# Issuing the second half-batch's v gathers in pairs, each pair behind a copy on GpSimd

## The chip, the core and the metric

The kernel runs on one core of a Trainium2 chip. The metric is the device time of one execution in microseconds (us), lower is better; the time of the kernel before is the median of three timed executions. The engines are named as in the profile: PE is TensorE (PEld its weight loads), DVE is VectorE, ACT is ScalarE, POOL is GpSimd, SP is SyncE.

## The reference, cut to what matters

Three parts run one after the other: an attention with decay, a mixture of experts, and a gated layer with a spatial mix. Only the last one is touched:

```python
def _moe2_ref(x, w_in, w_spatial, b_spatial, w_out):     # x: 4 x 576 x 512
    h = np.maximum(x @ w_in, 0.0)
    u, v = (h[..., :512], h[..., 512:])
    mu = np.mean(v, axis=-1, keepdims=True)
    var = np.mean((v - mu) ** 2, axis=-1, keepdims=True)
    v_n = (v - mu) / np.sqrt(var + 1e-06)
    v_s = np.einsum('ts,bsd->btd', w_spatial, v_n) + b_spatial[None, :, None]
    gated = u * v_s
    return gated @ w_out
```

## The kernel before

The tokens leave the experts sorted by expert. `project` computes u and v for 18 blocks of 128 sorted tokens and writes them to the DRAM tensors `z_u` and `z_v`. The spatial mix needs the tokens in their original order, so rows are fetched back with indirect DMAs that POOL issues (`gather`, L982: 128 rows of about 2 KB each, into a tile `vL` for v and `ug` for u).

The batch of four is worked in two half-batches, `m` = 0 and 1, of two batch elements each, `hf` = 0 and 1. A half-batch has nine v gathers (four blocks for each element and one block that holds the last 64 tokens of both). `norm_all` normalises a gathered v block and splits it in a high and a low part, so that three matmuls in place of one give full precision (`mm3`, L977). For each (m, hf), `mixed` (L1147) computes the spatial mix of a slice `f` of 128 features: two groups of 14 matmuls, one for 288 output tokens each, into two PSUM tiles `acc`. DVE then adds the bias and writes the sum into the tile `sb` (L1171). The steps for f = 0 to 3 follow each other.

At one of these steps (`f == at`) PE also transposes the gathered u rows (`tr_u`, L1144), ACT copies them to `u`, and the next u gathers are issued (`fetch_u`); they reuse the five `ug` tiles, so most wait for the transposes. From that step on `gate` (L1175) multiplies `sb` by u in place on DVE (L1177, and L1178 for the last 64 columns) and splits the product with ACT (L1179, L1180) and DVE (L1181, L1182). When both elements of a half-batch are through, `oproj` (L1184) multiplies by `w_out`: four blocks of the first element, one block `gm` with the last 64 tokens of both elements, four blocks of the second. For m = 0, the normalisation of the next half-batch's v rows runs beside these.

In this last part the order is written by hand (`tc.manual_schedule` for all engines): each engine executes its instructions in the order in which the code issues them. The nine v gathers of m = 1 are issued by one call, `raw1 = fetch_v(vnq, 1)` (L1221), right after the four u gathers of (m, hf) = (0, 1).

Of the kernel before, what the change touches and what calls it, by code (L numbers as in the profile page):

```python
# [8 lines left out]
F32 = mybir.dt.float32  # L9
# [15 lines left out]
P = 128  # L25
# [133 lines left out]
def fused(tc, blk, wgl, w1, w2, wv, wu, ws, wo, bs, cst, out, dbg=None, stop=9, caps=CAPS):  # L159
    nc = tc.nc  # L160
    V, A, G, T, SP = nc.vector, nc.scalar, nc.gpsimd, nc.tensor, nc.sync
    top = ExitStack()
    with top:
# [27 lines left out]
        def rpool(stack, name, bufs, **kw):  # L191
            return stack.enter_context(tc.tile_pool(name=name, bufs=bufs, reuse_waits="tile", side="right", **kw))
# [780 lines left out]
        smp = rpool(top, "smp", 4)  # L973
# [8 lines left out]
        def gather(src, j, t):  # L982
            G.indirect_dma_start(out=t.bitcast(F32), out_offset=None, in_=src[:],  # L983
                                 in_offset=bass.IndirectOffsetOnAxis(ap=yidx[:, j:j + 1], axis=0))

        def gather_v(pool, j, k):
            t = pool.tile([P, FH + (32 if k == 8 else 16)], F32R, name=f"vL{k}")[:, :FH + 2]
            gather(z_v, j, t)
            return t

        def scaled_rows(j, vL):
            mv = vL.bitcast(F32)[:, FH:]
            sd = smp.tile([P, 1], F32, name="sd")
            A.activation(sd, mv[:, 1:2], AF.Sqrt, scale=pr2[:, j:j + 1], bias=epst)
            yield
            rd = smp.tile([P, 1], F32, name="rd")
            V.reciprocal(rd, sd)
            V.tensor_tensor(rd, rd, pr_t[:, j:j + 1], op=ALU.mult)
            vn = vgp.tile([P, FH], F32, name="vn")
            V.tensor_scalar(vn, vL.bitcast(F32)[:, :FH], mv[:, 0:1], rd, op0=ALU.subtract, op1=ALU.mult)  # L1000
            yield vn

        def split_rows(pool, k, vL, vn):
            if k < 8:
                vH = pool.tile([P, FH], F32R, name=f"vH{k}")
                A.copy(vH, vn)
                yield
                V.tensor_tensor(vL[:, :FH], vn, vH.bitcast(F32), op=ALU.subtract)
                yield vH, vL
                return  # L1010
            stk = [pool.tile([P, FH], F32R, name=f"stk{hf}") for hf in range(2)]
            halves = [(stk[hf], slice(hf * 64, hf * 64 + 64), slice(64 - hf * 64, 128 - hf * 64)) for hf in range(2)]
            for t, sl, _ in halves:
                A.copy(t[sl], vn[sl])
            yield
            for t, sl, _ in halves:
                V.tensor_tensor(vL[sl, :FH], vn[sl], t[sl].bitcast(F32), op=ALU.subtract)
            yield stk
            for t, sl, ot in halves:
                A.dma_start(out=t[ot].bitcast(F32), in_=vL[sl, :FH].bitcast(F32))  # L1020

        def jof(m, hf, c):
            return 16 + m if hf == 2 else 4 * c + 2 * m + hf
# [3 lines left out]
        def units(m):  # L1027
            return [(hf, c, jof(m, hf, c), 8 if hf == 2 else 4 * hf + c) for hf, c in UNITS]

        def fetch_v(pool, m):  # L1030
            return [gather_v(pool, j, k) for _, _, j, k in units(m)]

        def norm_all(pool, m, raw, out_):
            prev = None
            late = iter(())
            for (hf, c, j, k), vL in list(zip(units(m), raw)) + [((None, None, None, None), None)]:
                if vL is not None:
                    sc = scaled_rows(j, vL)
                    next(sc)
                next(late, None)  # L1040
                if prev:
                    sp = split_rows(pool, prev[1], prev[2], prev[3])
                    next(sp)
                if vL is not None:
                    vn = next(sc)
                if prev:
                    out_[prev[0]] = next(sp)
                    late = sp
                prev = ((hf, c), k, vL, vn)
                yield  # L1050
# [78 lines left out]
        vnq = rpool(top, "vnq", 1)  # L1129
        ugp = lpool(top, "ugp", 5)  # L1130

        def fetch_u(m, hf):
            todo = [jof(m, hf, c) for c in range(4)] + ([16 + m] if hf == 0 else [])
            ugs = []
            for j in todo:
                ug = ugp.tile([P, FH], F32R, name="ug")
                gather(z_u, j, ug[:])
                ugs.append(ug)
            return ugs

        def tr_u(ug, dst):
            tp = trp.tile([P, 4, P], F32, name="tp", tag="tr")
            for f in range(4):
                T.transpose(tp.bitcast(F32R)[:, f, :], ug[:, f * P:(f + 1) * P], identR)  # L1144
            A.copy(dst, tp)  # L1145

        def mixed(hf, fs, vnt):  # L1147
            vm = vnt[2, 0]
            parts = [(f, t0) for f in fs for t0 in (0, 288)]
            accs = {p_: acp.tile([P, 512], F32, name="acc") for p_ in parts} if len(fs) > 1 else {}  # L1150

            def rows(p_, c):
                if p_ not in accs:
                    accs[p_] = acp.tile([P, 512], F32, name="acc")
                acc, ts, cols = accs[p_][:, :288], slice(p_[1], p_[1] + 288), slice(p_[0] * P, (p_[0] + 1) * P)
                if c < 4:
                    vH, vL = vnt[hf, c]
                    mm3(acc, vH[:, cols], vL[:, cols], wsH[c][:, ts], wsL[c][:, ts], c == 0, False)
                else:
                    T.matmul(acc, lhsT=vm[hf][:, cols], rhs=wsH[4][:, ts], start=False, stop=False)  # L1160
                    T.matmul(acc, lhsT=vm[hf][:, cols], rhs=wsL[4][:, ts], start=False, stop=True)  # L1161

            steps = [(p_, c) for c in range(5) for p_ in parts] if len(fs) > 1 else \
                [(p_, c) for p_ in parts for c in range(5)]
            for p_, c in steps:
                rows(p_, c)
            sbs = []
            for f in fs:
                sb = vsp.tile([P, S], F32, name="sb", bufs=4)
                for t0 in (0, 288):  # L1170
                    V.tensor_tensor(sb[:, t0:t0 + 288], accs[f, t0][:, :288], bst[:, t0:t0 + 288], op=ALU.add)  # L1171
                sbs.append((f, sb))
            return sbs
# [23 lines left out]
            return [(out[2 * m + hf, c * P:(c + 1) * P, :], 0, P)]  # L1197

        ugs = fetch_u(0, 0)
        for m in range(2):  # L1200
            gs = []
            gm = (mxp.tile([P, 4, P], F32R, name="gmH"), mxp.tile([P, 4, P], F32R, name="gmL"))
            um = mxp.tile([P, 4, P], F32, name="um")
            for hf in range(2):
                u = utp.tile([P, 4, 512], F32, name="u")
                g = (bgp.tile([P, 4, 512], F32R, name="bigH"), bgp.tile([P, 4, 512], F32R, name="bigL"))
                gs.append(g)
                at = 3 - hf if m == 0 else 0
                sbs = []
                for fs in ([(0, 1), (2,), (3,)] if m == hf == 0 else [(0,), (1,), (2,), (3,)]):  # L1210
                    f = fs[-1]
                    sbs += mixed(hf, fs, vnt)
                    if f == at:
                        for c in range(4):
                            tr_u(ugs[c], u[:, :, c * P:(c + 1) * P])
                        if hf == 0:
                            tr_u(ugs[4], um)
                        if (m, hf) != (1, 1):
                            ugs = fetch_u(m + hf, 1 - hf)
                        if m == hf == 0:  # L1220
                            raw1 = fetch_v(vnq, 1)  # L1221
                    if f >= at:
                        for f_, sb in sbs:
                            gate(hf, f_, sb, u, um, g, gm)
                        sbs = []
            norm = iter(())
            if m == 0:
                vnt = {}
                norm = norm_all(vnq, 1, raw1, vnt)
            for c in range(4):  # L1230
                oproj(jof(m, 0, c), *gs[0], c * P, blk_out(m, 0, c))
                next(norm, None)
            oproj(16 + m, *gm, 0, [(out[2 * m + hf, 512:576, :], hf * 64, 64) for hf in range(2)])
            for c in range(4):
                next(norm, None)
                oproj(jof(m, 1, c), *gs[1], c * P, blk_out(m, 1, c),
                      ((0, 256), (256, 256)) if m == 1 and c == 3 else ((0, 512),))
                next(norm, None)
# [22 lines left out]
```

## Time and profile before

| | us |
|---|---|
| median of three timed executions | 601.96 (600.61 to 602.49) |
| the profiled execution's own time | 598.48 |
| its span, first to last instruction | 596.7 |
| PE busy in the span | 572.8 (96%) |
| DVE, ACT, POOL busy | 358.9, 222.0, 213.8 |

The profile shows one execution. A row of the timeline gives the start and duration of an instruction, its engine, its line in the kernel and the tiles it writes and reads; brackets at the end hold the idle time of the engine before it and what ended it. "issue" there means that nothing in the profile explains the wait. The clock column is the granted TensorE clock as a share of 2.4 GHz. Times within the span are counted from its first instruction.

### The profile page before, as it was taken

What the parts mean: (1) busy time and instruction counts of PE and PEld (TensorE: products, weight loads), DVE (VectorE), ACT (ScalarE), POOL (GpSimd) and SP (SyncE); (2) the same over time, 40 slices, a digit from 0 to 9 for tenths busy, and PEclk for the clock granted to TensorE, in tenths of its full rate; (3) what the DMA queues carried; (4) which work ended last, traced back from release to release, by engine and by line L of the source; (5) the groups of instructions that cost most, each with busy time, mean ns of one, the idle gap of its engine ahead of it and who ended that gap; (6) DMA issues with size and microseconds to landing.
All of it is one profiled execution on the core that took longest, in us unless ns stands there. A gap on an engine that the chain in (4) does not pass through costs nothing. (4 is left out here: it accounts for less than half of the span.)

```text
span 596.7 us, 10499 instructions
## 1 busy us (share of the span) xinstructions
PE 572.8 (96%) x3903; PEld 520.5 (87%) x3903; DVE 358.9 (60%) x771; ACT 222.0 (37%) x461; POOL 213.8 (36%) x179
## 2 busy tenths in 40 slices
PE   8899999899999999999999999999999886999997
PEld 6789989559999999999999997888888885889986
DVE  2587577765466767879865434876643751765520
ACT  2121122226454545454555532222333431563322
POOL 4346544454334264646455130332005264102000
PEclk9899999899999999999999999999999996999999
DMA  9999996178754465467565423444425464332012
GB/s 280 343 303 304 286 266 197 64 245 273 256 177 151 142 206 159 161 230 217 173 197 173 145 60 108 142 124 147 129 108 169 151 184 131 125 112 84 1 71 88
DMA packets 44234, 102.65 MB, mean 172 GB/s; under 512 B 6316, under 2 KB 15916, under 8 KB 44176
## 3 DMA queue, kind: packets, MB, share of 16 engines
q1 hardware_dynamic: 37872, 82.15, 44.7%
q0 software_dynamic: 5984, 19.24, 10.2%
q8 instruction: 32, 0.52, 0.3%
q10 hardware_dynamic: 320, 0.52, 0.3%
q14 instruction: 26, 0.21, 0.1%
HBM read 82.18 MB, written 18.89 MB: 169 GB/s over the span
## 5 line engine op out<-in xcount | busy, mean ns | idle before, releaser
L810 POOL TENSOR_TENSOR wL<-wst,wH 128x1024 fp32r<-128x1024 f32 x23 | 58.3, 2533 | 65.0 <-ACT wH L809 57.9
L810 DVE TENSOR_TENSOR wL<-wst,wH 128x1024 fp32r<-128x1024 f32 x41 | 54.3, 1323 | 41.6 <-ACT wH L809 40.3
L823 PE MATMUL acc<-hL,wH 128*128 128x256 f32 (+7 forms) x256 | 78.2, 306 | 0.9 <-DVE hL L841 0.9
L822 PE MATMUL acc<-hH,wH 128*128 128x256 f32 (+7 forms) x256 | 78.9, 308 | 0.0
L823 PE MATMUL acc<-xL,wH 128*128 128x256 f32 (+7 forms) x256 | 77.9, 304 | 0.3 <-DVE xL L780 0.3
L822 PE MATMUL acc<-xH,wH 128*128 128x256 f32 (+7 forms) x256 | 77.9, 304 | 0.2 <-issue 0.2
L824 PE MATMUL acc<-xH,wL 128*128 128x256 f32 (+7 forms) x256 | 77.8, 304 | 0.0
L824 PE MATMUL acc<-hH,wL 128*128 128x256 f32 (+7 forms) x256 | 77.6, 303 | 0.0
L809 ACT CAST wH<-wst 128x1024 fp32r<-128x1024 f32 x64 | 65.0, 1051 | 14.1 <-DMA wst<-in_w 14.1
L823 PEld LDWEIGHTS acc<-hL,wH 128*128 128x128 f32 x256 | 48.1, 188 | 1.4 <-DVE hL L841 1.4
L822 PEld LDWEIGHTS acc<-xH,wH 128*128 128x128 f32 x256 | 48.1, 188 | 0.8 <-ACT xH L779 0.7
L823 PEld LDWEIGHTS acc<-xL,wH 128*128 128x128 f32 x256 | 48.1, 188 | 0.6 <-DVE xL L780 0.5
L822 PEld LDWEIGHTS acc<-hH,wH 128*128 128x128 f32 x256 | 48.1, 188 | 0.2
L824 PEld LDWEIGHTS acc<-hH,wL 128*128 128x128 f32 x256 | 48.1, 188 | 0.1
L824 PEld LDWEIGHTS acc<-xH,wL 128*128 128x128 f32 x256 | 48.1, 188 | 0.0
L317 PE MATMUL sc<-qz,blk 128*128 128x137 f32 x288 | 40.4, 293 | 3.1 <-DMA qz<-in_blk 2.5
L978 PE MATMUL acc<-wsH,vH 128*128 128x288 f32 x128 | 38.8, 303 | 3.2 <-ACT ze L1093 1.7
L979 PE MATMUL acc<-wsL,vH 128*128 128x288 f32 x128 | 38.7, 302 | 2.9 <-issue 2.9
L317 PEld LDWEIGHTS sc<-qz,blk 128*128 128x128 f32 x288 | 36.6, 196 | 5.0 <-issue 1.6
L860 ACT COPY yT<-acc 128x256 f32 (+7 forms) x32 | 13.4, 418 | 69.5 <-PE acc L824 66.7
L980 PE MATMUL acc<-wsH,vL 128*128 128x288 f32 x128 | 38.8, 303 | 0.4 <-issue 0.4
L840 ACT ACTIVATE hH<-acc 128x256 fp32r<-128x256 f32 (+7 forms) x64 | 26.4, 426 | 32.6 <-PE acc L824 32.5
(227 smaller groups left out, 1298.5 us busy)
## 6 DMA issues: line engine op xcount, KB each, us to landing
wst<-in_w SPq DMA_DIRECT2D x64, 512.0 KB
blk<-in_blk SPq DMA_DIRECT2D x18, 512.0 KB
blk<-in_blk SPq DMA_DIRECT2D x12, 548.0 KB
z_v<-ze SPq DMA_DIRECT2D x18, 257.0 KB
qz<-in_blk SPq DMA_DIRECT2D x36, 128.0 KB
z_u<-ze SPq DMA_DIRECT2D x18, 256.0 KB
out<-ob SPq DMA_DIRECT2D x15, 256.0 KB
raw<-in_wv SPq DMA_DIRECT2D x4, 512.0 KB
```

What stands on the lines that cost most here:

```text
L317: T.matmul(sv[:, i, :], lhsT=d["kv"][:, h, :], rhs=d["q"][h % 2][:, h // 2, :], start=True, stop=True)
L809: A.copy(wH, st)
L810: (G if u % 8 in LPOOL and u > 1 else V).tensor_tensor(wL, st, wH.bitcast(F32), op=ALU.subtract)
L822: T.matmul(acc, lhsT=wH, rhs=xH, start=first, stop=False)
L823: T.matmul(acc, lhsT=wH, rhs=xL, start=False, stop=False)
L824: T.matmul(acc, lhsT=wL, rhs=xH, start=False, stop=last)
L840: A.activation(hH[:, :C], acc[:, :C], AF.Relu)
L860: A.copy(yT[:, d, bass.ds(at, C)], acc[:, :C])
L978: T.matmul(acc, lhsT=lH, rhs=rH, start=first, stop=False)
L979: T.matmul(acc, lhsT=lH, rhs=rL, start=False, stop=False)
L980: T.matmul(acc, lhsT=lL, rhs=rH, start=False, stop=last)
```

## The change

The call that issued the nine v gathers at once is gone. In its place a generator, `fetch_v_behind`, issues two gathers at a time, each time after a copy on POOL of one column of an `sb` tile. It is advanced once after each of the four mix steps of (m, hf) = (0, 1), with the `sb` that this step wrote, and once more after the last gate of that element (column 575 of the last `sb`, after the gate has rewritten it), for the ninth gather. The copies write a 128x1 tile `pace`.

```diff
+        def fetch_v_behind(pool, m, out_):
+            todo = units(m)
+            while todo:
+                behind = yield
+                pace = smp.tile([P, 1], F32, name="pace", tag="rd")
+                G.tensor_copy(pace, behind)
+                for _, _, j, k in todo[:2]:
+                    out_.append(gather_v(pool, j, k))
+                todo = todo[2:]
...
         ugs = fetch_u(0, 0)
+        raw1 = []
+        paced = fetch_v_behind(vnq, 1, raw1)
+        next(paced)
...
                         if (m, hf) != (1, 1):
                             ugs = fetch_u(m + hf, 1 - hf)
-                        if m == hf == 0:
-                            raw1 = fetch_v(vnq, 1)
+                    if m == 0 and hf == 1:
+                        try:
+                            paced.send(sbs[-1][1][:, 575:576])
+                        except StopIteration:
+                            pass
+                    sb_last = sbs[-1][1]
                     if f >= at:
                         for f_, sb in sbs:
                             gate(hf, f_, sb, u, um, g, gm)
...
             if m == 0:
                 vnt = {}
+                try:
+                    paced.send(sb_last[:, 575:576])
+                except StopIteration:
+                    pass
                 norm = norm_all(vnq, 1, raw1, vnt)
```

On POOL this is the order of the gathers before, from the u gathers of m = 0 on (the first nine `ug`, five for hf 0 and four for hf 1, stand in one row; a number behind a name tells one tile from another):

```order
L983 DMA ug<-z_u,yidx 128x512 x9
L983 DMA vL_7170<-z_v,yidx 128x514
L983 DMA vL_7172<-z_v,yidx 128x514
L983 DMA vL_7174<-z_v,yidx 128x514
...
L983 DMA vL_7186<-z_v,yidx 128x514
L983 DMA ug<-z_u,yidx 128x512 x9
```

And this is the same place now:

```order
L983 DMA ug<-z_u,yidx 128x512 x9
L1038 COPY pace<-sb 128x1
L983 DMA vL_7232<-z_v,yidx 128x514
L983 DMA vL_7234<-z_v,yidx 128x514
L1038 COPY pace<-sb 128x1
L983 DMA vL_7271<-z_v,yidx 128x514
L983 DMA vL_7273<-z_v,yidx 128x514
L983 DMA ug<-z_u,yidx 128x512 x5
L1038 COPY pace<-sb 128x1
L983 DMA vL_7344<-z_v,yidx 128x514
...
L1038 COPY pace<-sb 128x1
```

Four v gathers now stand ahead of the five u gathers of (m, hf) = (1, 0) and five behind them, with five copies between.

On DVE no instruction is added or moved. These are the gates of the slices f = 0 to 2 of (m, hf) = (0, 1), with their waits, as they stood before:

```order
L1177 TENSOR_TENSOR sb<-sb,u 128x512 [waits DVE_49,Activation_49]
L1178 TENSOR_TENSOR sb<-sb,um 128x64
L1181 TENSOR_TENSOR bigL<-sb,bigH 128x512 [waits Activation_49]
L1182 TENSOR_TENSOR gmL<-sb,gmH 128x64 [waits Activation_49]
L1177 TENSOR_TENSOR sb<-sb,u 128x512
```

And as they stand now (the line numbers are ten higher):

```order
L1187 TENSOR_TENSOR sb<-sb,u 128x512 [waits DVE_49,Activation_49]
L1188 TENSOR_TENSOR sb<-sb,um 128x64 [waits Pool_49]
L1191 TENSOR_TENSOR bigL<-sb,bigH 128x512 [waits Activation_49]
L1192 TENSOR_TENSOR gmL<-sb,gmH 128x64 [waits Activation_49]
L1187 TENSOR_TENSOR sb<-sb,u 128x512
```

In each of the four slices the multiplication of the last 64 columns now waits for POOL, since the copy reads column 575 of the `sb` that it overwrites.

## Rows read from the trace of the kernel before

**Rows 1.** The page: each engine's busy time, share of the span, instructions.
```profile
PE 572.8 (96%) x3903; PEld 520.5 (87%) x3903; DVE 358.9 (60%) x771; ACT 222.0 (37%) x461; POOL 213.8 (36%) x179
```

**Rows 2.** Windows: stretch, length, busy time by engine, granted clock, DMA share, GB/s.
```profile
455.20:466.50 11.30, 9.86 (x46) 7.81 (x44) 7.91 (x22) 6.61 (x15) 7.05 (x7) 1.00 0.86 249
490.50:501.70 11.20, 4.89 (x19) 3.42 (x18) 1.82 (x6) 0.76 (x2) 6.68 (x8) 0.75 0.71 204
501.70:506.70 5.00, 5.00 (x30) 4.99 (x30) 1.60 (x4) 1.06 (x3) 0.82 (x1) 0.54 0.00 0
```

**Rows 3.** Timeline of PE, 480 to 512 us.
```profile
485.07 0.29 PE L1161 MATMUL acc<-wsL,stk 128*128 128x288 f32 x1
...
486.94 0.29 PE L1161 MATMUL acc<-wsL,stk 128*128 128x288 f32 x1
...
490.40 0.30 PE L980 MATMUL acc<-wsH,vL 128*128 128x288 f32 x1
491.62 0.29 PE L1160 MATMUL acc<-wsH,stk 128*128 128x288 f32 x1 [0.92 <-issue]
...
501.62 0.40 PE L978 MATMUL acc<-wsH,vH 128*128 128x288 f32 x1 [1.00 <-issue]
...
504.93 1.96 PE L1144 MATMUL tp<-identR,ug 128*128 128x128 f32 x16
506.73 0.36 PE L978 MATMUL acc<-wsH,vH 128*128 128x288 f32 x1
```

**Rows 4.** Timeline of POOL, 440 to 597 us.
```profile
452.12 0.98 POOL L983 DMA_INDIRECT vL<-z_v,yidx  x1 [40.05 <-issue]
...
463.13 0.95 POOL L983 DMA_INDIRECT vL<-z_v,yidx  x1 [0.30 <-issue]
...
481.60 0.94 POOL L983 DMA_INDIRECT ug<-z_u,yidx  x1 [1.60 <-PE tp L1144]
...
485.33 1.00 POOL L983 DMA_INDIRECT ug<-z_u,yidx  x1 [0.30 <-issue]
486.64 0.95 POOL L983 DMA_INDIRECT vL<-z_v,yidx  x1 [0.30 <-issue]
...
498.37 0.95 POOL L983 DMA_INDIRECT ug<-z_u,yidx  x1 [0.30 <-issue]
505.88 0.94 POOL L983 DMA_INDIRECT ug<-z_u,yidx  x1 [6.57 <-PE tp L1144]
```

**Rows 5.** DMA from 484 to 512 us: GB/s in 40 slices of 0.7 us.
```profile
GB/s 152 181 217 193 222 252 135 212 182 194 153 200 200 253 165 253 165 229 211 212 206 206 217 211 205 12 0 0 0 0 0 0 0 64 257 141 222 181 217 140
```

**Rows 6.** Chain that ended last, 470 to 597 us, pieces in order of time.
```profile
555.76 1.50 PE tp L1144 x16
```

**Rows 7.** Timeline of DVE, 462 to 597 us.
```profile
491.92 0.45 DVE L1171 TENSOR_TENSOR sb<-acc,bst 128x288 f32<-128x288 f32 x1
493.13 0.46 DVE L1171 TENSOR_TENSOR sb<-acc,bst 128x288 f32<-128x288 f32 x1 [0.76 <-PE acc L1161]
501.66 1.19 DVE L1171 TENSOR_TENSOR sb<-acc,bst 128x288 f32<-128x288 f32 x3 [8.07 <-PE acc L1161]
...
512.59 0.22 DVE L1178 TENSOR_TENSOR sb<-sb,um 128x64 f32<-128x64 f32 x1
...
514.10 0.82 DVE L1171 TENSOR_TENSOR sb<-acc,bst 128x288 f32<-128x288 f32 x2
...
528.94 0.69 DVE L1008 TENSOR_TENSOR vL<-vn,vH 128x512 fp32r<-128x512 f32 x1
```

**Rows 8.** Groups of instructions on POOL: count, busy us, mean ns, idle before.
```profile
L350 POOL TENSOR_TENSOR kt<-blk,c_ktab 128x512 f32<-128x512 f32 x16 | 16.9, 1056 | 19.5 <-DMA blk<-in_blk 18.3 <-DVE ua L446 1.2
...
L417 POOL MEMSET zero<- 128x8 f32 x1 | 0.1, 111 | 0.0
```

**Rows 9.** Timeline of ACT: two evictions of `oproj`, 12 matmuls apart.
```profile
574.01 0.69 ACT L1192 ACTIVATE ob<-acc,pr_t 128x512 f32<-128x512 f32 x1 [2.03 <-PE acc L980]
576.73 0.69 ACT L1192 ACTIVATE ob<-acc,pr_t 128x512 f32<-128x512 f32 x1 [2.03 <-PE acc L980]
```

## The prediction

> **What bounds the kernel now.** The page comes first: PE is busy in 96% of the span [rows 1], so a change that touches no matmul can only win where PE stands still or is slow. The windows find such a place. Between 490.5 and 501.7 us PE is busy for 4.89 of 11.2 us, and in the 5 us behind it its granted clock is 0.54 [rows 2], which means that it ran mostly at the lower level, 1.2 GHz. The timeline of PE shows what that is. Two groups of 14 matmuls end 1.87 us apart (485.07 and 486.94), 0.134 us for a matmul. At 490.40 the even row breaks: the next matmul starts at 491.62, and only from 501.62 on do they follow without gaps; the gaps are put down to "issue", so to no semaphore that the profile shows [rows 3].
>
> What went on beside it is on POOL and the DMA queues. Four u gathers start at 481.60, the nine v gathers at 486.64, one more u gather at 498.37 [rows 4]: fourteen in a row, one each 1.3 us. The traffic is about 200 GB/s in every slice until the one that begins at 501.5 (12 GB/s), then zero [rows 5]. PE runs again at 501.62, in that same slice. The stall is seen from DVE too: by the timeline of PE the second group of f = 0 was through at 486.94 + 0.29 = 487.2, but the addition that waits for it ran only at 493.13, with the wait put down to PE, and three more together at 501.66 after 8.07 us [rows 7]. So what PE finishes is reported late while the gathers run, and in the end PE itself hardly gets on. The profile names no cause; that the run of gathers is the cause is inferred from the common end.
>
> **What the stall costs.** From 490.40 to the first matmul behind the transposes, at 506.73, are 16.33 us. In them lie the matmul at 490.40 itself, 30 more of 0.134 us (2 that end f = 1, 28 of f = 2), 4.1 us in all, and 16 transposes; the same 16 took 1.50 us later, undisturbed [rows 6]. That ends at 496.0. The stage loses 506.73 - 496.0 = 10.7 us: about 9.0 until 501.62, and 1.7 in the slow clock behind it.
>
> **The change, part by part.** Nothing is computed less and no transfer is dropped.
>
> *The nine gathers move.* The last u gather before them is through on POOL at 485.33 + 1.00 = 486.3 [rows 4]. The next may start only when both additions of f = 0 are done. These stand on DVE behind the gates of the first element, so the first is at 491.92 as before [rows 7], and the second, no longer late, ends at about 492.8. So there is a break of 6.5 us in the gathers where there was none. In it PE runs f = 1 and most of f = 2; by the steps above its transposes end at 496.0, f = 3 (28 matmuls, 3.7 us) at 499.8, and then come the blocks of oproj, 2.72 us each [rows 9].
>
> *Five copies are added on POOL.* The trace has no such copy there. The nearest small row is a memset of 128x8, 0.11 us; far above lies a product of 128x512, 1.06 us [rows 8]. With 0.3 us between instructions that is 0.4 to 1.4 us for each; I take 0.45, since one column is close to the small row. In POOL's order: copy at 492.8, two v gathers (2.5 us at 1.25), copy, two more until 498.7, five u gathers until 504.95 (by then the transposes they wait for are past; before, they waited until 505.88 [rows 4]), copy until 505.4.
>
> *Four waits of DVE for POOL are added.* The costly one is the gate of f = 2: its L1178 waits for the third copy, which stands behind five u gathers. Before, L1178 ran 7.66 us after the transposes began, 512.59 against 504.93 [rows 3, 7]; without the stall that would be 494.5 + 7.7 = 502.2. Now it runs at 505.4, so DVE stands for 3.2 us. Queued behind it on DVE are the additions of f = 3, which followed 1.51 us after L1178 (514.10) [rows 7], now at 507.0 and 507.4. Who waits for these? The five PSUM tiles `acc` go round, so oproj's fourth block needs the first of them. PE reaches it at 499.8 + 3 x 2.72 = 507.9: 0.5 us to spare, cost zero. With the dear copy (three ahead of the wait, 0.9 more each) the addition ends at 510.1 and PE waits 2.2 us. Zero is what I take, 2.2 is kept for the range.
>
> *What else is later.* The ninth v gather is issued near 511. The normalisation of its row stands on DVE behind eight others. The fifth of the nine blocks, the last that the next mix needs at its start, was through at 529.6, 15.5 us after the additions of f = 3 [rows 7]; now that is 522.5, and PE comes to that mix at 499.8 + 9 x 2.72 = 524.3. Cost zero, covered by nine blocks of oproj; without them it would be the wait for a gather.
>
> **The sum.** 598.48 for the profiled execution, less 10.7, is 587.8. The median of the timed runs is 3.5 us above that execution; taking the same 10.7 from 601.96 gives 591.3 us.
>
> [...]
>
> **Rivals.**
>
> *The stall belongs to something else (no change).* PE might be held by its own instruction stream, or the recording of the profile might be what backs up; then timed runs have no such stall and the change buys nothing. For it: an earlier run of nine gathers, 452.12 to 463.13 [rows 4], shows no such collapse; PE was busy 9.86 of 11.30 us there, at full clock [rows 2]. Against the recording: the profiled execution is 3.5 us shorter than the median, not longer. If so, PE still reaches the transposes at 504.9, the third copy ends near 511, before L1178 at 512.59, and the new waits cost nothing: 602.0 us, 600.2 to 603.8.
>
> *The stall comes back in part.* Behind the break, 14 gathers follow nearly unbroken, from 493.3 to about 512. The earlier nine under 512-wide matmuls did little harm [rows 2], so I expect none there; but if half of the 10.7 comes back, it is 596.6 us (593.5 to 600).
>
> *The joined run of gathers stalls PE for longer (slower).* The u gathers of the next half-batch now lie between v gathers, and the run is longer than the old one behind its first four: it ends near 512 + 2.3 us for the last landing, 514. Onset decides. The old stall came 8.8 us after the run's first gather (481.60 to 490.40): then 502.2 to 514, 11.9 us, of which PE uses a fifth (16 matmuls of 0.134 in 11.2 us), 9.7 lost and again 1.7 in the slow clock: 11.4 against 10.7, 602.7 us. Counted from the first v gather it came after 3.8 us: then from 497.1, 16.9 us, 13.7 + 1.7 lost, 606.7 us. It is slower by over 0.3% if the stall lasts more than 13.5 us. Against it: from 499.8 on PE issues a matmul only each 0.227 us [rows 9], as in the earlier nine.
>
> **How the numbers follow.** Full relief 0.47, its own range 589 to 594 (the dear copies at the top, a little more relief at the bottom, if timed runs hold more stall than the profiled one); part of it 0.20; no change 0.21; slower 0.12. About 0.3% (1.8 us) is what a measurement can tell from no change: faster 0.67, same 0.21, slower 0.12. A range from 588.5 to 602.2 leaves out the slower case and the upper part of no change.
>
> **What will show it.** In the profile after, PE should have no "issue" gaps between the gates of the first element and the transposes, its clock should stay at 1.00 there, the transposes should begin near 494.5 instead of 504.9, and DVE should wait some 3 us for POOL at L1188 of f = 2. It is wrong if PE still stalls until the traffic ends, if gaps appear between 500 and 514 under oproj, if the copies cost over 1 us each, or if the profile is relieved and the timed runs are not.

## The result and the profile after

The changed kernel took 594.55 us (median of 4 runs, 591.37 to 598.1). The kernel before, run beside it, took 601.29 us (4 runs, 599.1 to 602.49). The ratio is 0.9897 [0.9864, 0.9931], a gain of 6.2 us with an interval of 4.1 to 8.2. The profiled execution took 594.42 us, its span is 592.4 us. How much of this belongs to the change and how much to the conditions of the measurement is the subject of the experiments: in two of their four measuring sessions the kernel before took 589 us by itself.

First the page's line of engines (busy time, share of the span, instructions), to be read beside [rows 1]:

```profile
PE 571.1 (96%) x3903; PEld 518.9 (88%) x3903; DVE 360.1 (61%) x771; ACT 221.7 (37%) x461; POOL 216.1 (36%) x184
```

The work is the same but for five instructions on POOL, the copies. PE has the same 3903 matmuls. So the windows have to show where the time went. The columns are those of [rows 2]: stretch, length, busy time of PE, PEld, DVE, ACT and POOL, granted clock, DMA share, GB/s.

```profile
490.50:501.70 11.20, 11.13 (x89) 10.75 (x88) 6.91 (x18) 4.33 (x10) 3.89 (x6) 1.00 0.33 83
501.70:506.70 5.00, 5.00 (x33) 4.61 (x32) 3.84 (x9) 1.56 (x5) 4.01 (x4) 1.00 0.74 206
511.00:517.00 6.00, 5.06 (x21) 3.60 (x21) 3.21 (x10) 2.58 (x7) 3.80 (x5) 1.00 0.52 134
```

Between 490.5 and 501.7 us PE now works through: 11.13 of 11.20 us, with 89 matmuls where there were 19, at full clock. The last row is new: between 511 and 517, under `oproj`, PE stands for almost a microsecond. The timeline of PE shows both:

```profile
489.43 0.29 PE L1171 MATMUL acc<-wsL,stk 128*128 128x288 f32 x1
...
491.30 0.29 PE L1171 MATMUL acc<-wsL,stk 128*128 128x288 f32 x1
...
499.18 1.67 PE L1154 MATMUL tp<-identR,ug 128*128 128x128 f32 x16
500.68 0.37 PE L978 MATMUL acc<-wsH,vH 128*128 128x288 f32 x1
...
510.40 0.39 PE L980 MATMUL acc<-woH,bigL 128*128 128x512 f32 x1
...
511.31 0.39 PE L980 MATMUL acc<-woH,bigL 128*128 128x512 f32 x1
512.31 0.40 PE L978 MATMUL acc<-woH,bigH 128*128 128x512 f32 x1 [0.61 <-issue]
513.03 0.48 PE L979 MATMUL acc<-woL,bigH 128*128 128x512 f32 x1 [0.33 <-issue]
...
514.43 0.39 PE L978 MATMUL acc<-woH,bigH 128*128 128x512 f32 x1
```

The first two rows are the two group ends that stood at 485.07 and 486.94 before [rows 3] (the line numbers are ten higher). From the first of them to the first matmul behind the transposes there are 500.68 - 489.43 = 11.25 us now, and 506.73 - 485.07 = 21.66 us before: 10.4 us less. The gap under `oproj` is the same kind of gap as in [rows 3], put down to "issue". Ten matmuls lie between the starts at 510.40 and 514.43; at 0.227 each, the pace of [rows 9], they would take 2.27 us and not 4.03. So 1.8 us come back there.

Starts of the same matmul in both traces, counted from the first one, give the account of the whole execution (worked out from the records, not a view of the profile):

```
matmul   before    after   difference
  1000   111.76   115.00   +3.24
  3200   471.67   476.79   +5.12
  3300   485.07   489.43   +4.36
  3340   490.40   494.74   +4.34
  3400   508.51   502.47   -6.04
  3450   518.45   514.19   -4.26
  3902   592.83   588.58   -4.25
```

The first 3.2 us are lost in the attention, far ahead of anything that the change touches; another execution of the same changed kernel (e6, below) has +1.2 there. So the two profiled executions differ by 4.3 us in span, while the change itself makes 10.4 less 1.8, that is 8.6 us, between matmul 3300 and the end.

On POOL the copies stand as the order said:

```profile
490.18 0.94 POOL L983 DMA_INDIRECT ug<-z_u,yidx  x1 [0.30 <-PE acc L1171]
497.59 0.18 POOL L1038 COPY pace<-sb 128x1 f32<-128x1 f32 x1 [6.46 <-DVE sb L1181]
497.93 0.97 POOL L983 DMA_INDIRECT vL<-z_v,yidx  x1 [0.15 <-issue]
...
509.32 0.20 POOL L1038 COPY pace<-sb 128x1 f32<-128x1 f32 x1
...
510.95 0.95 POOL L983 DMA_INDIRECT vL<-z_v,yidx  x1 [0.31 <-issue]
513.54 0.70 POOL L1038 COPY pace<-sb 128x1 f32<-128x1 f32 x1 [1.64 <-issue]
...
517.06 0.97 POOL L983 DMA_INDIRECT vL<-z_v,yidx  x1 [0.16 <-issue]
```

Behind the last u gather POOL stands 6.46 us. Then 11 gathers follow without a break (497.93 to 511.90), four of v, five of u, two of v. A copy takes 0.18 to 0.27 us, but one of the five, the fourth, 0.70. On DVE:

```profile
509.55 0.23 DVE L1188 TENSOR_TENSOR sb<-sb,um 128x64 f32<-128x64 f32 x1 [2.82 <-POOL pace L1038]
...
510.45 0.45 DVE L1181 TENSOR_TENSOR sb<-acc,bst 128x288 f32<-128x288 f32 x1
513.01 0.46 DVE L1181 TENSOR_TENSOR sb<-acc,bst 128x288 f32<-128x288 f32 x1 [2.12 <-remote]
```

The gate waits 2.82 us for the third copy. The third row is a late report as in [rows 7]: the last matmul of that group began at 504.33 and took 0.29 us by PE's timeline, and the addition ran only at 513.01, 8.4 us later. For 2.12 us of these DVE stood ready and waited. The profile puts the wait down to "remote", that is, it finds no engine that ended it; the instruction waits for the same semaphore as the additions of [rows 7], whose waits are put down to PE.

### The profile page after: what moved, and what is told of

The parts are those of the page before. It is cut to its first block, busy times and chain, and to the rows that moved or that the text cites. A ratio compares the mean times of both kernels' runs of the same rounds, so it can differ in the third digit from the quotient of the medians.

```text
span 592.4 us, 10505 instructions
## 1 busy us (share of the span) xinstructions
PE 571.1 (96%) x3903; PEld 518.9 (88%) x3903; DVE 360.1 (61%) x771; ACT 221.7 (37%) x461; POOL 216.1 (36%) x184
## 3 DMA queue, kind: packets, MB, share of 16 engines
q0 software_dynamic: 5984, 19.24, 10.4%
## 5 line engine op out<-in xcount | busy, mean ns | idle before, releaser
L860 ACT COPY yT<-acc 128x256 f32 (+7 forms) x32 | 13.4, 418 | 69.5 <-PE acc L824 66.7
```

What stands on the lines that cost most here:

```text
L860: A.copy(yT[:, d, bass.ds(at, C)], acc[:, :C])
```

## The experiments

**What is tested.** Theory A is the prediction's: the run of gathers that POOL issues holds PE, not the bytes that they move and not the place in the program. Its rivals: the bytes do it; the stall belongs to PE's own instructions at that place; it is in the recording of the execution. Of the 1.8 us under `oproj` there are two readings: J, the joined run of gathers stalls PE again, and W, DVE's wait for the third copy (2.82 us) delays the additions for which PE then waits. Twelve runs in four sessions; a session is a group of kernels measured together on one chip, the kernel before among them.

What came out first has to be told first, since no number can be read without it: **the stall was there in two of the four sessions and not in the other two**. The kernel before, run beside them, took 589.24 us (31 runs) and 588.46 us (29 runs) in two sessions, 600.58 us (13 runs) and 600.65 us (7 runs) in the other two. The mean granted clock of its timed runs was 0.993 and 0.994 in the first two, 0.985 and 0.986 in the others, so the difference is in all the timed runs and not in the profiled one alone. The experiments stand below by session. The kernel before has no trace from a session without the stall; that PE doesn't stand there is read from its times and from the traces of the variants.

### First session: the stall is not there (before: 589.24 us)

**e1_plain.** The nine v gathers become plain transfers that SP issues in the same place. They bring neighbouring rows in place of the wanted ones, so the kernel computes with other rows.

```diff
+        def load_v(pool, m):
+            ts = []
+            for _, _, j, k in units(m):
+                t = pool.tile([P, FH + (32 if k == 8 else 16)], F32R, name=f"vL{k}")[:, :FH + 2]
+                G.memset(t.bitcast(F32)[:, :1], 0.0)
+                SP.dma_start(out=t.bitcast(F32), in_=z_v[j * P:(j + 1) * P, :])
...
-                            raw1 = fetch_v(vnq, 1)
+                            raw1 = load_v(vnq, 1)
```

> The kernel before, but the nine v gathers are plain transfers from SP's queue, of the same size into the same tiles, started at the same place (a one-column memset on POOL holds each back). The rows are not the wanted ones: each tile gets 128 neighbouring rows. Theory A (it is the run of gathers issued on POOL that holds PE, not the bytes): the four u gathers are then a run of four, PE has no issue gaps in the second element's mix, the stage is 10 us shorter, about 591 us. Theory B (the traffic itself holds PE): the same bytes move at the same place, the gaps stay as long as the traffic lasts, 5 to 9 us lost, 596 to 601 us. Theory C (the stall has nothing to do with either): 601 us.

Measured: 587.16 us, ratio 0.998 [0.9951, 1.0009].

**e2_late.** All nine gathers stand behind the mix, in one run, behind one copy.

```diff
-                        if m == hf == 0:
-                            raw1 = fetch_v(vnq, 1)
...
+                pace = smp.tile([P, 1], F32, name="pace", tag="rd")
+                G.tensor_copy(pace, sb_last[:, 575:576])
+                raw1 = fetch_v(vnq, 1)
                 norm = norm_all(vnq, 1, raw1, vnt)
```

> The kernel before, but all nine v gathers stand behind one copy after the last gate of the second element, under oproj; DVE waits for no copy before that. Theory A: the mix is free of the stall as in the changed kernel (10 us), five u gathers are followed by nine v gathers; if only an unbroken run of about nine or more stalls PE, a gap of 1 to 3 us as at 511 us in the changed kernel or none comes back, 592 to 595 us. Rival: a run of nine under oproj stalls PE like under the mix, or the normalisation comes too late for the next mix: 598 to 602 us.

Measured: 588.81 us, 0.9988 [0.9954, 1.0022].

**e3_split.** Five gathers in the old place, without copies; four behind the mix.

```diff
                         if m == hf == 0:
-                            raw1 = fetch_v(vnq, 1)
+                            raw1 = [gather_v(vnq, j, k) for _, _, j, k in units(1)[:5]]
...
+                G.tensor_copy(pace, sb_last[:, 575:576])
+                raw1 += [gather_v(vnq, j, k) for _, _, j, k in units(1)[5:]]
```

> The kernel before with five of the nine v gathers in the old place and four behind the last gate. The run behind 481.6 us is then ten gathers in place of fourteen and ends about 5 us earlier. Theory A with the length of the run as what counts: the stall begins at the same place, 8 to 9 us after the run's first gather, and ends with the traffic near 497 us: half of it stays, 595 to 597 us. Rival: below some number of gathers nothing happens at all: 591 to 592 us.

Measured: 588.4 us, 0.9992 [0.9963, 1.002].

**e4_spaced.** The order of before, with two memsets of 128x512 on POOL behind each v gather, so that fewer gathers are issued in a time.

```diff
-                            raw1 = fetch_v(vnq, 1)
...
+                            for _, _, j, k in units(1):
+                                raw1.append(gather_v(vnq, j, k))
+                                G.memset(spin, 0.0)
+                                G.memset(spin, 0.0)
```

> The kernel before with two memsets of a private tile on POOL behind each of the nine v gathers (about 0.55 us each), so that they come every 2.4 us instead of every 1.3 and the stretch with gathers is longer, 486 to 508 us. Theory A in the form that only an unbroken run holds PE: each gather has landed before the next starts, no stall, 591 to 593 us. Rival (any gather beside the mix costs PE its share): about the same loss spread over a longer stretch, 599 to 602 us.

Measured: 588.19 us, 0.9989 [0.9964, 1.0014]. That each gather has landed before the next starts is not shown: the 18 v gathers of both half-batches have a median of 3.8 us from issue to landing in this trace.

None of the four can be told from the kernel before, and all expectations that took a stall in it for granted fall: there was none to take away. The trace of e3_split says more. The window, and two rows of POOL:

```profile
484.00:506.00 22.00, 22.00 (x151) 20.69 (x150) 14.98 (x38) 8.44 (x22) 12.31 (x13) 1.00 0.54 147
```

```profile
480.12 0.95 POOL L983 DMA_INDIRECT ug<-z_u,yidx  x1 [0.75 <-PE tp L1144]
...
492.19 0.95 POOL L983 DMA_INDIRECT ug<-z_u,yidx  x1 [0.30 <-PE acc L1161]
```

Ten gathers in a row (four u, five v, one u) beside the mix, 13 us, and PE is busy 22.00 of 22.00 us. In the kernel before, with the stall, PE broke 8.8 us after the first gather of such a run [rows 3, 4]. So in the first session a run of gathers did not hold PE.

### Second session: both kernels again (before: 600.58 us)

**e5_before_again** and **e6_after_again** are the kernel before and the kernel after, unchanged.

> The kernel before, unchanged, with a profile of its own. In the four experiments above the kernel before took 589.2 us where it had taken 601.3, so the stall may be no fixed property of the kernel. If the 12 us between are the stall (theory A with a condition outside the kernel), this profile has no issue gaps in the second element's mix when the time is near 589, and has them when it is near 601. Rival: the stall is there in both, and the 12 us come from another stage.

> The changed kernel, unchanged, beside the kernel before on one chip. If the stall is there (before near 601): 593 to 596 us as recorded. If it is not (before near 589): nothing to win; the new wait of DVE for POOL costs nothing as worked out, so the same within 0.3%, 588 to 590 us; rival: the wait of the fourth block of oproj for the late additions costs 1 to 3 us, 590 to 592 us.

Measured: e5 599.19 us, 0.9992 [0.9958, 1.0027]; e6 592.78 us, 0.9859 [0.9806, 0.9913], a gain of 8.5 us (5.2 to 11.7), just under the 593 to 596 us that were expected. The stall is back. In e5's windows, in PE's timeline and in the line of GB/s from 484 to 512 us (40 slices of 0.7 us):

```profile
490.50:501.70 11.20, 7.32 (x43) 6.11 (x42) 4.45 (x12) 1.53 (x4) 8.49 (x9) 0.91 0.72 204
501.70:506.70 5.00, 3.87 (x20) 3.38 (x19) 1.28 (x3) 0.53 (x2) 0.80 (x2) 0.51 0.38 110
```

```profile
493.29 0.29 PE L1161 MATMUL acc<-wsL,stk 128*128 128x288 f32 x1
...
493.82 0.29 PE L978 MATMUL acc<-wsH,vH 128*128 128x288 f32 x1
494.37 0.29 PE L979 MATMUL acc<-wsL,vH 128*128 128x288 f32 x1 [0.26 <-issue]
...
504.31 0.40 PE L978 MATMUL acc<-wsH,vH 128*128 128x288 f32 x1 [0.33 <-issue]
```

```profile
GB/s 240 76 0 164 228 164 228 170 211 228 211 229 123 241 141 241 153 229 153 247 147 282 200 241 200 206 217 193 205 29 0 0 0 0 105 258 152 222 135 252
```

Two things are to be seen. The last gap ends at 504.31, in the slice from 504.3 to 505.0 in which the traffic falls from 205 to 29 GB/s: the common end of [rows 3, 5] a second time. And the gaps begin at another instruction: in f = 2, four matmuls behind the end of f = 1 at 493.29, while in [rows 3] they begin two matmuls ahead of that end. A stall that belonged to PE's instructions at a place would begin at the same one. It is also shorter: by the starts of the same matmuls, from the 3300th to the last, e5 takes 2.1 us less than the trace of before.

In e6 the gap under `oproj` is there again:

```profile
508.40 0.40 PE L980 MATMUL acc<-woH,bigL 128*128 128x512 f32 x1 [0.91 <-issue]
509.11 0.49 PE L978 MATMUL acc<-woH,bigH 128*128 128x512 f32 x1 [0.31 <-issue]
```

By the starts of the same matmuls e6 loses 2.0 us there, after 10.4 gained ahead of it (from +0.6 to -9.8 against the trace of before, then to -7.8).

### Third session: three of the variants with the stall there (before: 600.65 us)

**e7_plain_again**, **e8_spaced_again** and **e9_late_again** are the kernels of e1, e4 and e2. This is the chip of the first session, so the condition doesn't go with the chip.

> The kernel of e1 once more (nine plain transfers in place of the nine v gathers; the rows are not the wanted ones), since where e1 ran the kernel before had no stall to lose. What counts is the kernel before beside it. If that is near 600: theory A (gathers issued on POOL hold PE) gives about 590 and no issue gaps in the second element's mix; theory B (the traffic holds PE, whoever issued it) gives 595 to 600 with gaps while the nine transfers run. If the kernel before is near 589: no difference, as in e1.

> The kernel of e4 once more (two memsets on POOL behind each of the nine v gathers, one gather each 2.4 us). With the kernel before near 600: theory A (an unbroken run is needed) gives 590 to 593 and no gaps; the rival (the number of gathers counts, not their spacing) leaves gaps of some 9 us in the mix and under oproj, 598 to 601. Near 589: no difference.

> The kernel of e2 once more (all nine v gathers in one run behind the last gate of the second element, no wait of DVE for POOL before). With the kernel before near 600: the mix is free of the stall (10 us); as the changed kernel had a stall of 2 us under oproj after some ten gathers in a row, a run of nine behind five u gathers should cost 1 to 3 us there: 591 to 594, level with the changed kernel. Rival: the run of nine under oproj stalls PE for its whole length, 597 to 600. Near 589: no difference.

Measured: e7 589.54 us, 0.9805 [0.9744, 0.9866]; e8 591.21 us, 0.9831 [0.977, 0.9893]; e9 591.93 us, 0.9841 [0.9779, 0.9903].

e7, the window of the old stall and SP's issues:

```profile
490.50:501.70 11.20, 11.20 (x90) 11.00 (x89) 6.95 (x18) 4.31 (x10) 3.42 (x13) 1.00 0.88 288
```

```profile
491.30 5.31 SPq L1038 DMA_DIRECT2D vL<-z_v  x9
```

Nine transfers of the same size in the same place, 288 GB/s where the stalling kernel had 204 [rows 2], and PE doesn't stand at all. The bytes are not it; what is left is what comes with the indirect transfers that POOL issues.

e8, the same window and two neighbouring gathers:

```profile
490.50:501.70 11.20, 11.15 (x88) 10.80 (x87) 7.06 (x18) 4.14 (x11) 10.08 (x15) 1.00 0.51 140
```

```profile
492.78 0.95 POOL L983 DMA_INDIRECT vL<-z_v,yidx  x1 [0.15 <-issue]
...
495.01 0.95 POOL L983 DMA_INDIRECT vL<-z_v,yidx  x1 [0.16 <-issue]
```

All nine are in the old place, one each 2.23 us in place of 1.3, and the stall is gone. So it is not enough that the gathers lie beside the mix; in the third session they stalled PE only where they followed each other closely. That was done without any wait on the work of PE or DVE.

e9, a window under `oproj` and the first and last of the nine gathers:

```profile
511.00:523.00 12.00, 12.00 (x54) 9.95 (x53) 6.13 (x18) 6.50 (x14) 9.15 (x10) 1.00 0.74 219
```

```profile
511.53 0.97 POOL L983 DMA_INDIRECT vL<-z_v,yidx  x1 [0.15 <-issue]
...
521.93 1.02 POOL L983 DMA_INDIRECT vL<-z_v,yidx  x1 [0.30 <-issue]
```

Nine in a row under `oproj` cost PE nothing, with a break of 5.21 us on POOL ahead of their copy. The 1 to 3 us that were expected there did not come, though the time lies in the range given. This speaks for J in the matter of the 1.8 us: `oproj` bears a run of nine, and in the changed kernel the gap came at the end of eleven without a break (PE's even row ends with the matmul at 511.31, 13.4 us after the first of them at 497.93). It doesn't show it alone, since e9 has no wait of DVE for a copy either.

e7, e8 and e9 don't come down to the times of the same kernels in the first session: 589.54 against 587.16 us, 591.21 against 588.19, 591.93 against 588.81. So 2.4 to 3.1 us of the 11.4 us between the two sessions stay when the stall is gone; what they are is not shown.

### Fourth session: to tell J from W; the stall is not there (before: 588.46 us)

**e10_after_third** is the changed kernel, unchanged; **e12_spaced_third** is e4 once more. **e11_ahead** puts the third copy and its pair ahead of the five u gathers:

```diff
+                        if m == 0 and hf == 1:
+                            paced.send(sbs[-1][1][:, 575:576])
                         if (m, hf) != (1, 1):
                             ugs = fetch_u(m + hf, 1 - hf)
-                    if m == 0 and hf == 1:
+                    if m == 0 and hf == 1 and f != at:
```

> The changed kernel, unchanged, to be compared on one chip with the two below. With the kernel before near 600: 592 to 594 us, with a gap of about 2 us on PE under oproj. With the kernel before near 589 (no stall to lose): theory: the added copies and waits cost nothing, 588 to 590; rival: the late additions of the last slice hold oproj's fourth block, 590 to 592.

> The changed kernel with the third copy and its two v gathers ahead of the five u gathers, not behind them. DVE no longer waits 3 us for POOL at the gate of f = 2; the run of gathers is as long as before, six v, five u, then the rest. Theory J (the 2 us on PE under oproj are the joined run of gathers): the gap stays, 592 to 595 us. Theory W (they are the price of DVE's wait): the gap goes, about 2 us faster than the changed kernel, 590 to 591.

> The nine v gathers spaced by memsets on POOL (as e4 and e8), beside the changed kernel on one chip. Theory J: with no unbroken run there is no gap under oproj, 1 to 2 us faster than the changed kernel, 590 to 592 us with the kernel before near 600. Rival: level with it.

Measured: e10 588.42 us, 1.0001 [0.998, 1.0022]; e11 588.14 us, 1.0002 [0.9976, 1.0028]; e12 588.21 us, 1.001 [0.9986, 1.0034]. All three are within 0.3% of before, and neither e11 nor e12 could tell what it was made for. But e10's trace answers the question of W from the other side. Two windows, and DVE's wait:

```profile
490.50:501.70 11.20, 11.19 (x91) 11.02 (x90) 6.85 (x19) 4.35 (x10) 5.22 (x8) 1.00 0.32 86
...
507.00:511.00 4.00, 4.00 (x19) 3.30 (x19) 3.38 (x9) 1.85 (x6) 3.18 (x5) 1.00 0.73 204
```

```profile
506.93 0.23 DVE L1188 TENSOR_TENSOR sb<-sb,um 128x64 f32<-128x64 f32 x1 [2.82 <-POOL pace L1038]
...
507.83 0.81 DVE L1181 TENSOR_TENSOR sb<-acc,bst 128x288 f32<-128x288 f32 x2
```

The same wait of 2.82 us, and both additions of f = 3 run right behind the gate: no late report, and no gap of PE under `oproj`. So the wait alone costs PE nothing. The place of the gap speaks against W too. PE would wait for a PSUM tile that the additions free at the first matmul of a block of `oproj`, and a block has 12; the gap at 512.31 stands ahead of the seventh matmul of the third block (`oproj` begins at 504.47), the one of e6 at 508.40 ahead of the sixth. So W falls. In the fourth session the same order of the same gathers also gives no gap, so the 1.8 us go with the same condition as the 10.4. From the 3300th matmul to the last, e10 takes 10.65 us less than the trace of before, the changed kernel 8.61 us less in its own trace and 8.43 in e6.

A second mark of the condition is in the list of DMA issues (count, median us from issue to landing). Of the changed kernel in the session with its result, and of e10:

```profile
wst<-in_w SPq DMA_DIRECT2D x64, 512.0 KB
...
vL<-z_v,yidx POOLq DMA_INDIRECT x18
```

```profile
wst<-in_w SPq DMA_DIRECT2D x64, 512.0 KB, 3.8
...
vL<-z_v,yidx POOLq DMA_INDIRECT x18, 4.2
```

The landing times are missing for every transfer of the program, plain ones from SP too, in the traces of before, after and e5 to e9; in those of e1 to e4 and e10 to e12 nearly all are there. The reason can be counted in the packed traces (worked out from the records, not a view of the profile): they hold the semaphore updates that come from a DMA, and of these the seven traces without the stall's condition have 5002 to 5008, the other seven 4196 to 4321 (before 4224, after 4252). The program does not make the difference: e4 and e8 are one kernel with 5003 and 4245, e2 and e9 one with 5004 and 4196. Between 480 and 520 us, where the gathers lie, e4 has 468 and e8 178. So about one record in seven is lost in the sessions with the stall, and there alone. The loss by itself doesn't stall PE, since e7, e8 and e9 lose as many and PE runs on. But a condition of the recording is the one thing seen here that parts the two kinds of session.

A late fetch of PE's instructions would be one more guess at the stall, and no record shows one: in the trace of before the two queues that the page calls "instruction" (32 packets in all on q8, 26 on q14) move one packet between 471 and 516 us, at 488.2, in 0.96 us, and the same 16 KB take 0.95 us in e4 and in e10.

## Why the prediction came out right, and what it had wrong

**The stall and its end.** Right where the stall exists. The stage was to lose 10.7 us less; it lost 10.4 less in the profiled execution and about as much less in e6. In e10, where nothing comes back, it is 10.65 by the matmul starts, so the size was right. The transposes were to begin near 494.5 in the time of before: 499.18 less the 4.34 us by which that execution was late is 494.8. The "issue" gaps are gone from the stage and its clock is 1.00. In the trace of before the clock has two values, 1.00 and 0.50: it is 0.50 in each us from 498 to 506, and there a matmul of 288 columns comes each 0.24 us (502.05 to 504.69), 1.2 columns per ns. At 1.00 one of 288 takes 0.134 us and one of 512 takes 0.227, so 2.4 columns per ns for the columns between. The 2.4 and 1.2 GHz of the clock are an estimate from these steps, one column to a cycle. That the gathers make the stall, which the prediction only inferred from the common end [rows 3, 5], is now shown for the sessions with the stall: e7 takes the gathers out of it and keeps more traffic, e8 keeps all of them in place and only spreads them, and either frees PE.

**The sum.** Predicted 591.3 us, measured 594.55: the gain is 6.2 us and not 10.7. The mis-sized term is the run behind the break. The prediction put nothing there in its likeliest case ("the earlier nine under 512-wide matmuls did little harm, so I expect none there"), and gave half of the 10.7 to the rival in which the stall comes back in part. It came back with 1.8 and 2.0 us: the mechanism of that rival, at a third of its size. That makes 8.6 us for the change in the profiled execution: inside the interval of the second session, 5.2 to 11.7 us, and just over that of the result, 4.1 to 8.2 us. The rest of the difference to 594.55 is not traced. Executions differ, by 3.2 us in the attention for example; and the slowest of the four timed runs, 598.1 us, has a granted clock of 0.985, as the kernel before has with its stall, against 0.990 to 0.997 in the other three, so more may have come back there.

**What was luck.** The range, 588.5 to 602.2 us, holds the forecast's likeliest case (591.3), the partial return (596.6) and no change (602.0), so the time alone proves none of them. The likeliest case, full relief, did not come; a smaller form of the partial return, which had 0.20, did. And no term of the prediction foresaw a state without the stall: measured in the fourth session, the changed kernel's 588.42 us would have been no change against the kernel before, and just under the range.

**Why the return is small.** The rival of the longer stall let it last to the end of the run, near 514 us in the time of before; its 2.3 us for the last landing are an estimate, from the end of the last gather at 499.32 to 501.62, where PE goes on [rows 3, 4]. The stall ended sooner, and the rows fit a loop: the held report delays the addition to 513.01, the fourth copy reads its sum and so begins only at 513.54, right behind it, and POOL issues no gather from 511.90 until then. The pacing breaks the run itself, and PE goes on. In e6 PE goes on by 509.11 and the copy there begins at 509.65. This is read from times that follow each other, not tried: no run takes the fourth copy away.

**The copies and the wait of DVE.** 0.45 us for a copy was high for four of the five: 0.18 to 0.27 us, and 0.34 us from the first copy's start to the next gather; the fourth took 0.70 and 0.86 us. The break was forecast at 6.5 us and is 6.46. DVE's wait for the third copy was forecast at 3.2 us and is 2.82; its cost of zero for PE is shown by e10, and by the place of the gap.

**The rival by the recording.** The prediction held against it that the profiled execution was shorter than the median of the timed ones. That reason is worth nothing: each timed run here comes with its span and granted clock too, so each leaves records of some kind. And two things speak for it that were not known then: the stall is there in some sessions and not in others, and in exactly those where it is, about one record of a landing in seven is missing. Neither says which is the cause of which. Every execution here left records, so whether the stall exists in one that leaves no record stays open, as does what decides the condition: one chip gave both. What is shown is that in these sessions the stall needs the close run of gathers.

**What that means for the change.** Where the stall is, it gains 6 to 9 us. The sessions differ by 11 to 12 us (600.6 less 588.5 to 589.2), but of these 2.4 to 3.1 stay in the kernels that have no stall, so the stall itself is worth some 8 to 11 us: 10.7 in the trace of before, 8.5 in e5 (10.65 less 2.1). Where it isn't, the change gains nothing and costs nothing: 1.0001 [0.998, 1.0022]. If the stall belongs to the recording, it gains nothing in an execution that isn't recorded; no run here tells. The three simpler ways out, plain transfers, spread gathers and the late run, stood at 589.5 to 591.9 us beside 600.65, and the changed kernel at 592.78 beside 600.58; the intervals overlap, so none of them is shown to be better.

## What to carry to other kernels

When PE's even row of matmuls breaks with "issue" gaps that no semaphore explains, compare its end with the end of what other engines issue; then take the suspect away while its bytes stay (e7), and spread it in place (e8). Before a stall is priced, the kernel before should be timed in a second session, and the trace looked through for records that are missing: here a term of 10.7 us, all that the change was worth, was there in one session and absent in the next. And a run of gathers that is moved joins the next run; its length behind the move is what has to be counted (here eleven in a row, with 1.8 us lost at their end).

## What the runs showed of the hardware that was not expected

- A dense run of gathers issued by POOL, one each 1.3 us, came in two of the four sessions, and in the result's, with late reports of PE's finished matmuls (8.4 us in the changed kernel) and then with gaps of PE. Counted to the last matmul in even row, the gaps began 8.8 us (before) and 9.4 us (e5) after the run's first gather beside matmuls of 0.134 us, and 13.4 us (after) and 12.9 us (e6) beside those of 0.227 us; with one gather each 2.23 us, none came.
- Nine plain transfers at 288 GB/s in the same place left PE busy 11.20 of 11.20 us.
- The same kernel on the same chip took 589.24 us (median of 31) in one session and 600.65 us (median of 7) in another.
- In the sessions with the stall, and only there, the traces lack about one in seven of the semaphore updates of landing DMAs (4245 against 5003 for one kernel), and the profile then gives no landing time for any transfer.
